# Eleven units of three heads instead of sixteen of two, in a kernel of two interleaved memory-attention layers

## The chip, the core and the metric

The kernel runs on one core of a Trainium2 chip. A core has five engines that run their own instruction streams and wait for each other through semaphores: TensorE (PE, matrix products; PEld is its weight loads), VectorE (DVE), ScalarE (ACT), GpSimd (POOL) and SyncE (SP, which only issues transfers). The metric is the time of one execution on the device in microseconds. Three timed runs of the kernel before took 1757.47 us in the median (1755.57 to 1760.67).

## The reference

A model of two layers, each an attention with a recurrent memory and then a gated feed-forward, on 2048 tokens of width 512, in bf16:

```python
def _A_ref(x, mem0, Wq, Wk, Wv, Wo, seg_len):      # 32 heads of 128, M = 8 memory rows, seg_len = 32
    mem = mem0
    for s in range(n_seg):                          # 64 segments, one after another
        h = jnp.concatenate([mem, xs], axis=1)      # 8 + 32 = 40 rows
        q, k, v = h Wq, h Wk, h Wv                  # per head
        scores = jnp.where(mask, q k^T * scale, -1e9)
        o = softmax(scores) v, then Wo
        mem = o[:, :M, :]; outs.append(o[:, M:, :])
def _B_ref(x, w_gate, w_up, w_down):
    return (_sigmoid(x w_gate) * (x w_up)) w_down   # hidden width 1792
x = x + A(layernorm(x)); x = x + B(layernorm(x))    # layer 1
x = x + A(layernorm(x)); x = x + B(layernorm(x))    # layer 2, same weights
```

The memory rows that a segment's attention puts out are the first rows of the next segment, so the 64 segments of a layer are a chain.

## The kernel before, in words

Both layers run interleaved: layer 2 follows layer 1 by `LAG` = 6 segments. There are 70 steps; step t does segment t of layer 1 and segment t - 6 of layer 2, side by side as 80 columns (2 x 40). The first six and the last six steps have one layer only, 40 columns. `emit_step` (line 743) writes one step. All attention weights stay in SBUF; the feed-forward weights stream from HBM by GpSimd (lines 1037, 1038, 1062) every time `ffn` (line 998) handles a block of four segments.

**A step.** The 32 heads are taken in six groups (line 379): a unit is the pair of heads k and 16 + k, a group is three units, and the last group is one unit. For each group: Q and K of three heads at a time (line 820, four matmuls per head and matrix), a ScalarE copy to `qku`, the scores (line 855), then on VectorE and ScalarE mask, maximum, difference, exponential, sum, reciprocal and product (lines 869 to 886). The product goes to `pb`, each head in 64 columns of which 40 are used, so that two heads side by side fill 128. One transpose per unit (`ptr`, line 898) turns [80 x 128] into [128 x 80], also in one-layer steps, where only 40 of the 80 columns are wanted.

Then the two heads of a unit have to be kept apart for one common matmul with V. Two copies, `spread` (line 903), write `ptsb` as a block diagonal: the first takes rows 0 to 39 as they are, the second takes rows 0 to 103 with a per-row factor (`self.lower`, 0 for rows below 64, 1 above), so that zeros stand above the second head's block. `pvm` (line 925) multiplies: per unit and layer one matmul with 104 rows (40 + 24 unused + 40) and 80 columns, the weights being a piece of `vsb`. The result is copied to `otsb`, and line 943 adds Wo over all heads in one bank, `WB`. The memory rows in it are copied (lines 956, 961) into `hT` for the next step.

**V rows.** `vsb` has on its rows the keys of a segment: 40 for the first head of each unit, from row 64 on 40 for the second, and 1024 columns (eight heads) per half; a step takes two halves out of a ring of three (`NV`, line 421). The rows have two sources. V of most input rows is known long before: `v_pass` (line 599), `v_half` (636) and `v_strip` (666) compute it for whole blocks, and write it to a scratch tensor `scr` in HBM; line 789 reads it back, per layer and half two transfers, eight in a two-layer step. V of the memory rows and eight input rows is computed in the step itself by `strips` (line 724, matmuls at line 734), copied to the tile `sst`, and spread from there by line 800, one transfer per layer and block of eight heads, again eight in a two-layer step. All of line 789 and 800 are issued by SyncE. PV of a unit waits for both kinds in its half.

**Order.** Nothing is scheduled at run time. `trace` puts down all tasks with what they read and write; `plan` (line 242) takes their order from the packed text `SEQUENCE`, which also has one bit for each task that may run on either of two engines (ACT or DVE, or SP or POOL). Each engine then executes its tasks in that order. `replay` works out from modelled durations how transfers are paced; `warm` (line 325) puts matmuls on zeros (`hot`, line 1162) into modelled gaps early on. PSUM has eight banks, shared by all products.

At the beginning `load_weights` (line 488) brings Wv, then Wq, Wk and Wo in three batches of heads, while x blocks are normalised and their V rows go to the scratch.

Of the kernel before, what the change touches and what calls it, by code (L numbers as in the profile page):

```python
# [19 lines left out]
P = 128  # L20
# [33 lines left out]
;Az(@{9OPHfC}>o!3$&_>1cSGYy1w~*vKE?LoDUO!`XV%;;<878Kns_@I+iX(74V;U`D{e|Ct%0x6blOT;$DygtQ>WP_y0Zcs7M#8ZgxUzzs1BnG}%%cF5wibfz3Qe?%`=oGh%zVh=;yB58Og*`2$-%qT7YV)FI3#cQ^-I`x  # L54
&G{OfvfRK6T<NC@t+QdCx)4z22oURtuAXpAF|V^CA{0!Ao{;`#`yj1}i}Ch1r!j#UV(;CNGol)x2h`J)DP9<BIpIsggIr#a!ba?+s&P#^RrmvVPy2*cyt7ch@zX6gEG&YI)o)JH5iL)7^9(PB6)!dAz;Y>UB@c<YVrN*C$bk
`UBwxs%kJ&?H?qYss(T75_dqsan*LzmQ){N;jUfw1c#CWqehzA$bo--AB9!AL8|W%F))ViX;pkqiEd(%YsDHo*bQ+Dg|=KU)AQj+ks~~@3^wm`_dZc8XZ*mz}(B-?_G(C#8p|4$Q#jx3XS>_o;hPB%dYQC+~oqb=g0I%bKtG
rSyhjEKC+rbuKFU;PbVGyzF>7DXS4Dk(aL?0A6S7iKWJkuCsaZ&wNS??_ECKySWtgC`xDEZU7C!<AWxdzXj9U63NE>5Yc6MUM!7}k$&z&CD4Mla1DpWf(QeoFAc7y6O-ohA*ItoS2?=lJ@>LMq|C7o-Q8n#{?T6q|_($+pX6
_0p%s=*z9d@;E{BD!r4PB$D?4z4z;XM@A#gsbsw%iD9{;3M*L!&6|ltPpFZQTPfqi^op#C!}qxPUz6u}3{jgHF!ebPiVZgXqS03CQ8v-k^3u$xlzD)_nJq?>hx&T8b)Jx{V$$2*B5>5^-kIDbQ&(GA|hBP)=(F?%hkS#wDGT
#CgyK0Y5|l(;pl7Bm@Ae`Cyw<S6@#gvE3~Ltq-@hCG>dDXcDc%GIkP2+V$B{Y>_nQ!q=}&Y+eo3QV2~`flzV#9vZJ2FD(Zk$8y(4#}Gzn2=SG;2y@jmsXC~$pqizsS*wm@&w7Uemq&=!vw#M0gE>GU>#$Al_0&=9s7POC5w8
wCVt2dTrQcn;ydUO5caqQt6VFB?-M8;1Ij6Y~M34Ev7kYUxYI$|K2JNpoTCmkHk{v}Wa!DAN((%u!t;57gvoi1te}1KiaM<<Va7#z02ym&DO$`u$X-wNEhOCQmVMW5<OAt7`JQGSmyI;Fyvnh!4?T{@zS!O)ZV>{z{r&tN&O  # L60
GBcSt6qX}d8a@4cOwmdsxK@1Mv#YW7t`b1`tw8V7V$oq81-WwoNwK3hAbp_&Ys1}c-<U=_9c;uuhJNYdr`2njZZKcwlt>88tzHvO<Nw5)Ia)x)ih?ng+Q@u-1OY<8L7mfOLpjHniZZD8P~1DNqhyvLy*LY_DO!$iQvIF_03_
EE9^VE0M=lc09iWqK)*H(FN&wXUGRX5gsbTWY``n1P4gcn)QJkM!Iu6;e3IY1dX)C1c=g)b8a@WC_r^F=YXB~yd>RICxRDT#R?s3pwyYelZ~(Od=uW_AQ|iZ{J?O2Am?k$-NCs+M8c1q6!k?FG0iDOdDLy%rHBg8)hQ4+1-z
R@{Ap_p0pz2P$nvy9rmW#FlW6F73m@h@<*e%j$nj_5%VAco?ETMr0eZ8Xy!ug=sl2$=fEr(So8hOJjcF6~Y#gB(6Vk!U4p28BbPQF;9$eSp3>(2rofD%eIS4Bc`-i8r`jjAPY>>>+KN(2@?36~@jFQW+GNvKz@40>EqjZYO|
77iYTi^gp5gp<lX+CRHkg_c+NPMgLuKp~|RIx%VhyA`P5<f^cxq>-JHS#&X5OH08lau6tLMOd>6r9lh*>|n+|+zk|ZVu}uQCdbU|W0?3WPkvHZ05nA&gswskrIp9CwZvW<S;hgUNw8j9H~ri&@R3`gYkPqser(Gw_2?=sq;T
y!hDzC8@%U)2fOR|h!v&I<K``c))TWKf3ngkKJ8>2Px^zg{R-tySFsSs(ViW4Mg5E8eo;c0H_qUP>?X8C3ZLi2Y>4oZp*rb^2xUJpiPqU1@@f!(!Z)ujbMCs8jDY(7I2P#e*mF`S@c#VZ<oZF}8WM<UftqDN4%J*(@+;wKru
&(Tm7u}Lr!6j(z$eS-xqe=3E7~&mY%i~Pr0J>Z)oX3f4M3a>RN4NT){|o2~R2gALm^t!8(ySW99ZkQ1^Mcvtk<kcIG;)P3;TII7uxp3TN|Op2#w{XqT5mmQW)a7oA=p7LL4FK9k9=P=qkq>Wz=Mx2PY99!w^_{^AvWc3$n%)
j;66<cd`~YkPDsPxCgft~&{c40sfzWb8^PRKCrLGR2ZwGeABQkk-tfoQtzz~DB(L@wF2kmrai9Yz9rw=m(z7Zw4~vQWSOjZ#;%i!*8A}~%D<yc5shh!vHK(ToI(Scm4-?@}3ByBLIf*T)P{h5e1`3IDo283%H7tZ0Y2N$!;`
# [293 lines left out]
class Kern:  # L361
    def __init__(self, ctx, tc, x_in, mem0, Wq, Wk, Wv, Wo, w_gate, w_up, w_down, out, lag=6, ring=8):
# [14 lines left out]
        assert ring > lag and lag >= BLK + 1  # L377
        self.NSTEPS = self.NSEG + lag
        self.scale = float(DH) ** -0.5
        self.HH = H // 2  # L380
        self.groups = []
        for u in range(0, self.HH, 3):
            us = list(range(u, min(u + 3, self.HH)))
            self.groups.append(([h for k in us for h in (k, self.HH + k)], us))
# [103 lines left out]
    def load_weights(self):  # L488
# [10 lines left out]
        for h0, n in ((0, 4), (4, 4), (8, 4), (12, 4), (16, 4), (20, 4), (24, 4), (28, 4)):  # L499
            cs = slice(h0 * P, (h0 + n) * P)  # L500
            tk = ld(self.wv[:, :, cs], wv_v[:, :, cs], P * self.DC * n * P * 2, [("wv", h) for h in range(h0, h0 + n)], [("wv", h0 - 8)] if h0 > 4 else [])
            if h0 > 4:
                tk.after = pl.writer[("wv", h0 - 8)]
# [738 lines left out]
```

## Time and profile before

| | |
|---|---|
| median of three timed runs | 1757.47 us |
| profiled execution, device time | 1760.81 us |
| its span, first to last instruction | 1759.0 us |
| instructions | 92161 |
| TensorE clock granted | 1.00 |
| moved by transfers | 273.42 MB, 155 GB/s |
| transposes, line 898 | 1120 |
| PV matmuls, line 925 | 2048 |
| scratch reads into `vsb`, line 789 | 508 |
| strip transfers into `vsb`, line 800 | 516 |

How to read a page. A line of groups has the source line, the engine and operation, what is written and read, the count, then busy time and the mean length of one in ns. Matmuls overlap in the pipeline, so the mean length of one (some 200 ns) isn't what it costs: that is the distance between starts, which the timeline shows. A line of waits has who waited, for whom, us in total, times, and the longest. SPq and POOLq are the queues of SyncE and GpSimd. Windows (from:to in us) give each engine's busy time in a stretch. "issue" as a releaser means that nothing in the profile explains the idle time.

### The profile page before, as it was taken

To read this page: it belongs to the slowest core of one execution; us is meant where nothing else is said; L and a number is where in the kernel's file an instruction comes from. 1 tells how busy PE (TensorE), PEld (TensorE's weight loads), DVE (VectorE), ACT (ScalarE), POOL (GpSimd) and SP (SyncE) were. 2 spreads that over 40 slices of the span, in tenths; PEclk is the share of its full clock that TensorE was granted. 3 is DMA by queue.
4 is the path that set the end of the run, shared out by engine and by line. 5 is a ranking of instruction groups with operands and counts; after the bars stand their busy time and mean duration, and the time that the engine had idled before them with its cause. 6 is when DMAs were issued, how large, how long until landed. Compare 5 with 4: busy or idle time off the path is not lost.

```text
span 1759.0 us, 92161 instructions
## 1 busy us (share of the span) xinstructions
PE 1742.0 (99%) x40015; PEld 1503.4 (85%) x40015; DVE 1233.3 (70%) x4096; ACT 1113.6 (63%) x2946; POOL 570.8 (32%) x818
## 2 busy tenths in 40 slices
PE   9999999999999999999999999999999999999998
PEld 4688788888898888989898888988888898988887
DVE  6577777676767776776677667667766776677766
ACT  4576777666566655666666667656666666666564
POOL 4312133423233233323333242323234232332433
PEclk9999999999999999999999999999999999999999
DMA  8934455645555455545555463545456454554554
GB/s 292 311 105 131 119 165 149 194 128 141 142 153 155 139 167 142 171 119 157 152 153 164 133 194 105 158 141 175 127 157 186 131 151 133 151 164 126 158 151 127
DMA packets 136128, 273.42 MB, mean 155 GB/s; under 512 B 30706, under 2 KB 69498, under 8 KB 135722
## 3 DMA queue, kind: packets, MB, share of 16 engines
q0 software_dynamic: 55680, 180.73, 35.5%
q1 hardware_dynamic: 80042, 86.79, 17.2%
q8 instruction: 314, 5.14, 1.3%
q14 instruction: 92, 0.75, 0.1%
HBM read 221.78 MB, written 27.07 MB: 141 GB/s over the span
## 4 chain that ended last, share of the span: by engine, by line
PE 94%; DMA 3%; SPq 1%; issue 1%; DVE 0%; ACT 0%; POOL 0%; DVEq 0%; POOLq 0%; ACTq 0%
PE bank L820 33%; PE bank L943 17%; PE bank L1045 11%; PE bank L734 7%; PE bank L609 7%; PE bank L1068 6%; PE bank L855 4%; PE bank L925 4%; PE bank L898 2%; PE bank L569 1%; DMA wq_sb<-in_A_Wq_dram 1%; DMA vsb<-sst 1%; SPq L800 1%; DMA wk_sb<-in_A_Wk_dram 1%; PE bank L1013 0%
## 5 line engine op out<-in xcount | busy, mean ns | idle before, releaser
L820 PE MATMUL bank<-hT,wk_sb 128*128 128x80 bf16 (+3 forms) x8960 | 616.2, 198 | 4.5 <-issue 3.1
L820 PE MATMUL bank<-hT,wq_sb 128*128 128x80 bf16 (+3 forms) x8960 | 615.9, 198 | 2.8 <-DMA wq_sb<-in_A_Wq_dram 1.5
L1176 ACT CAST qku<-bank 128x480 bf16<-128x480 f32 (+4 forms) x770 | 383.5, 507 | 272.8 <-PE bank L820 244.5
L820 PEld LDWEIGHTS <-wq_sb 128*128 128x128 bf16 x8960 | 453.7, 99 | 30.7 <-issue 14.0
L820 PEld LDWEIGHTS <-wk_sb 128*128 128x128 bf16 x8960 | 447.1, 99 | 4.0 <-issue 2.5
L869 DVE TENSOR_TENSOR st<-bank,cst 40x240 f32<-40x240 f32 (+3 forms) x768 | 280.1, 368 | 122.5 <-PE bank L855 108.2
L943 PE MATMUL bank<-otsb,wo_sb 128*128 128x80 bf16 (+1 forms) x8960 | 363.2, 198 | 0.6 <-issue 0.6
L943 PEld LDWEIGHTS <-wo_sb 128*128 128x128 bf16 x8960 | 335.1, 99 | 11.4 <-issue 1.3
L1062 POOL DMA_DIRECT2D wd<-in_B_w_down_dram x217 | 154.7, 713 | 354.6 <-PE bank L1068 85.6
L1038 POOL DMA_DIRECT2D wu<-in_B_w_up_dram x217 | 164.4, 758 | 298.9 <-PE bank L1045 94.3
L1176 ACT CAST otsb<-bank 128x480 bf16<-128x480 f32 (+3 forms) x420 | 199.9, 483 | 93.8 <-PE bank L925 58.3
L1037 POOL DMA_DIRECT2D wg<-in_B_w_gate_dram x217 | 164.0, 756 | 244.0 <-PE bank L1045 108.2
L879 ACT ACTIVATE st<-st 80x240 f32<-80x240 f32 (+3 forms) x420 | 158.9, 381 | 66.2 <-DVE st L876 63.1
L1045 PE MATMUL bank<-xnT,wg 128*128 128x128 bf16 (+2 forms) x1784 | 171.7, 218 | 0.5 <-issue 0.5
L1045 PE MATMUL bank<-xnT,wu 128*128 128x128 bf16 (+2 forms) x1784 | 171.1, 218 | 0.0
L881 DVE TENSOR_REDUCE small<-st 80x6 f32<-80x240 f32 (+3 forms) x420 | 151.0, 361 | 24.8 <-ACT st L879 22.2
L855 PE MATMUL bank<-qku 128*128 128x80 bf16 (+1 forms) x2240 | 160.7, 198 | 0.4 <-ACT qku L1176 0.4
L876 DVE TENSOR_TENSOR st<-st,small 80x240 f32<-80x240 f32 (+3 forms) x420 | 154.5, 370 | 6.6
L886 DVE TENSOR_TENSOR pb<-st,small 80x240 bf16<-80x240 f32 (+3 forms) x420 | 153.8, 370 | 6.1
L874 DVE TENSOR_REDUCE small<-st 80x6 f32<-80x240 f32 (+3 forms) x420 | 151.6, 363 | 6.7
L925 PE MATMUL bank<-ptsb,vsb 104*128 104x80 bf16 x2048 | 139.3, 199 | 2.2 <-DMA vsb<-sst 1.6
L855 PEld LDWEIGHTS <-qku 128*128 128x128 bf16 x2240 | 114.2, 99 | 30.1 <-ACT sst L1176 5.5
(107 smaller groups left out, 2330.7 us busy)
## 6 DMA issues: line engine op xcount, KB each, us to landing
wg<-in_B_w_gate_dram POOLq DMA_DIRECT2D x220, 256.0 KB, 4.3
wu<-in_B_w_up_dram POOLq DMA_DIRECT2D x220, 256.0 KB, 4.3
wd<-in_B_w_down_dram POOLq DMA_DIRECT2D x220, 256.0 KB, 4.0
vsb<-scr SPq DMA_DIRECT2D x460, 48.0 KB
vsb<-sst SPq DMA_DIRECT2D x464, 32.0 KB
scr<-vst SPq DMA_DIRECT2D x120, 96.0 KB
wv_sb<-in_A_Wv_dram SPq DMA_DIRECT2D x8, 512.0 KB
wo_sb<-in_A_Wo_dram SPq DMA_DIRECT2D x10, 384.0 KB
```

Source lines behind the costliest of these rows:

```text
L820: nc.tensor.matmul(o_ap, lhsT=W[:, c, h * P:(h + 1) * P], rhs=mv(c), start=(c == 0), stop=(c == DC - 1))
L855: nc.tensor.matmul(s_all(SB)[:, w0 + i, :], lhsT=fview(qku[:, i, 0, 0:1], [(1, P)]), rhs=qku[:, i, 1, 0:ncol], start=True, stop=True)
L869: pl.add("DVE", dve_ns(n, True), lambda gsz=gsz, hs=hs, st=st, SB=SB, pj_=pj_, npj_=npj_, mk=mk, idx=idx: nc.vector.tensor_tensor(out=st[p ...
L876: pl.add("DVE", dve_ns(n), lambda gsz=gsz, hs=hs, st=st, mx=mx: nc.vector.tensor_tensor(out=st[pr, hs], in0=st[pr, hs], in1=mx[pr, hs].uns ...
L879: pl.add("ACT", act_ns(n), lambda hs=hs, st=st: nc.scalar.activation(out=st[pr, hs], in_=st[pr, hs], func=ACTF.Exp, scale=self.scale), r=s ...
L925: nc.tensor.matmul(fview(OB[:, o:o + 1], [(ncol, 2), (1, L)]), lhsT=self.vsb[halves[u // 8]][0:64 + L, j, (u % 8) * P:(u % 8 + 1) * P], rh ...
L943: nc.tensor.matmul(WB[:, c * ncol:(c + 1) * ncol], lhsT=self.wo[:, h, c * P:(c + 1) * P], rhs=otsb[:, hl, 0:ncol], start=(h == 0 and c == ...
L1037: pl.add("POOL", 760, lambda wg=wg, fs=fs: nc.gpsimd.dma_start(out=wg[:], in_=self.wgv[:, :, fs]), r=[("wo", self.H - 1)], w=[gk] + bt, la ...
L1038: pl.add("POOL", 760, lambda wu=wu, fs=fs: nc.gpsimd.dma_start(out=wu[:], in_=self.wuv[:, :, fs]), r=[("wo", self.H - 1)], w=[uk] + bt, la ...
L1045: nc.tensor.matmul(gu[:, 2 * i + k, 0:n], lhsT=W[:, c, i * P:(i + 1) * P], rhs=xnT[:, c, rw], start=(c == 0), stop=(c == DC - 1))
L1062: pl.add("POOL", 760, lambda wd=wd, ip=ip: nc.gpsimd.dma_start(out=wd[:], in_=self.wdv[:, 2 * ip:2 * ip + 2, :]), w=[dk] + (["boot"] if se ...
L1176: nc.scalar.copy(out=dst, in_=src)
```

## The change

Units have three heads: k, 11 + k and 22 + k. There are eleven; the last has two heads. A group has two units, so group sizes stay six heads, five times, and then two. `pb` has three heads of 40 columns side by side (120 of 128); one transpose per unit, of as many columns as the step has. `spread` runs once per head place of the unit, three times in a full group, the second and third scaled by their own 0/1 factor. PV has 120 rows and 120 columns. `vsb` has one whole buffer per step (11 x 128 columns), two of them; its rows have no gap, so the filling with zeros at the beginning goes away.

V is stored in an order of its own: the first eight heads of each of the three rows, then the remaining 3, 3 and 2. `runs` cuts a stretch of stored columns into pieces that are contiguous in the scratch. Scratch reads are one transfer per layer and row, and strip transfers two (k = 0 for the first eight units, k = 1 for the others); both may be issued by SyncE or GpSimd, as a bit in the new sequence says. The sequence is new as a whole.

```diff
+        self.NU = (H + 2) // 3
+        self.row_heads = [list(range(i * self.NU, min((i + 1) * self.NU, H))) for i in range(3)]
         self.groups = []
-        for u in range(0, self.HH, 3):
-            us = list(range(u, min(u + 3, self.HH)))
-            self.groups.append(([h for k in us for h in (k, self.HH + k)], us))
+        for u in range(0, self.NU, 2):
+            us = list(range(u, min(u + 2, self.NU)))
+            self.groups.append(([r[k] for k in us for r in self.row_heads if k < len(r)], us))
...
-        self.NV = 3
+        self.NV = 2
-        self.vsb = [c.tile([P, 2, 1024], BF16, name=f"vsb{i}") for i in range(self.NV)]
+        self.vsb = [c.tile([P, 2, self.NU * P], BF16, name=f"vsb{i}") for i in range(self.NV)]
-        self.pb = [c.tile([LW, HG, 64], BF16, name=f"pb{i}") for i in range(3)]
-        self.ptsb = [c.tile([P, HG, 2, L], BF16, name=f"ptsb{i}") for i in range(3)]
+        self.pb = [c.tile([LW, 2, P], BF16, name=f"pb{i}") for i in range(3)]
+        self.ptsb = [c.tile([P, 2, 2, 3, L], BF16, name=f"ptsb{i}") for i in range(3)]
...
-        nc.vector.memset(self.lower, 1.0)
-        nc.vector.memset(self.lower[0:64], 0.0)
+        for i in (1, 2):
+            nc.gpsimd.memset(self.lower[i], 1.0)
+            nc.gpsimd.affine_select(out=self.lower[i], in_=self.lower[i], pattern=[[0, 1]],
+                                    compare_op=ALU.is_ge, fill=0.0, base=-i * L, channel_multiplier=1)
...
-        for k, t_ in enumerate(self.vsb):
-            pl.add("ACT", 1760, lambda t_=t_: (t_[32:64], fview(self.hot[32:64, 0:1], [(0, 2), (0, 1024)])),
...
+    def runs(self, k, w):
+        out = []
+        for i, r in enumerate(self.row_heads):
+            n = len(r) - 8
+            for p0, m, s0 in ((0, 4, 8 * i), (4, 4, 8 * i + 4), (8, n, 24 + 3 * i)):
+                lo, hi = max(s0, 4 * k), min(s0 + m, 4 * (k + w))
+                if lo < hi:
+                    h = r[p0 + lo - s0]
...
+                        out.append(((lo - 4 * k) * P, h * P, (hi - lo) * P, keys))
...
-        full = slice(0, LW)
+        full = slice(0, ncol)
...
-            for hf, vh in enumerate(halves):
-                for i in range(0 if j and not s else 2):
...
-                    pl.add("SP", 430, lambda j=j, s=s, row=64 * i + row + lo, h0=h0, vh=vh, r0=s * XS + lo, nx=nx: nc.sync.dma_start(
...
+            for i, rh in enumerate(self.row_heads):
...
+                pl.add(("SP", "POOL"), {"SP": 430, "POOL": 590}, lambda j=j, row=L * i + row + lo, h0=rh[0], m=m, r0=s * XS + lo, nx=nx: (
+                    "dma", self.vsb[vh][row:row + nx, j, 0:m], self.scr[j][r0:r0 + nx, h0 * P:h0 * P + m]),
...
+            for k in (0, 1):
...
+                    for i in range(3):
+                        p0, o, m, c = (32 * i, 0, self.full, 0) if not k else (96, 3 * P * i, (len(self.row_heads[i]) - 8) * P, self.full)
+                        pl.add(("SP", "POOL"), {"SP": 632, "POOL": 640}, lambda p0=p0, o=o, m=m, c=c, i=i, j=j, lo=lo, k0=k0, nr=nr: (
...
-                           r=kk, w=[(qku, "e")], use=[qku])
+                           r=kk + hkeys, w=[(qku, "e")], use=[qku])
...
-                    nc.tensor.transpose(out=pt[:, ul * LW:(ul + 1) * LW], in_=pb[full, 2 * ul:2 * ul + 2, :].rearrange("p i k -> p (i k)"),
+                    nc.tensor.transpose(out=pt[:, ul * LW:ul * LW + ncol], in_=pb[full, ul, :],
                                         identity=self.ident[full, full])
...
-            for i in (0, 1):
+            for i in range(ni):
                 def spread(i=i, nu=nu, ptsb=ptsb, PB=PB):
-                    r = slice(0, 64 * i + L)
+                    r = slice(0, L * (i + 1))
...
-                                         lhsT=self.vsb[halves[u // 8]][0:64 + L, j, (u % 8) * P:(u % 8 + 1) * P],
-                                         rhs=ptsb[0:64 + L, ul * nj + idx, :, :], start=True, stop=True)
+                                         lhsT=self.vsb[vh][0:L * ni, j, u * P:(u + 1) * P],
+                                         rhs=ptsb[0:L * ni, ul, idx, 0:ni, :], start=True, stop=True)
```

`load_weights` also changes: Wv comes in ten pieces in the new stored order instead of eight, and Wq, Wk and Wo in batches of 2, 4 and 5 units, each as three pieces, one per row of heads. In `v_pass`, `v_half` and `v_strip` each write to the scratch becomes one write per piece that `runs` returns.

306 lines of the change are left out of this document (159 added, 147 removed).

## The prediction

> **What bounds the kernel now.** First the page's busy shares and the table by stage, to see which engine has no room left; the last columns are granted clock, DMA share and GB/s.
>
> ```profile
> PE 1742.0 (99%) x40015; PEld 1503.4 (85%) x40015; DVE 1233.3 (70%) x4096; ACT 1113.6 (63%) x2946; POOL 570.8 (32%) x818
> ...
> 0.00:90.00 90.00, 84.76 (x1125) 48.14 (x1126) 53.01 (x159) 47.50 (x115) 34.57 (x78) 1.00 0.91 296
> 90.00:195.00 105.00, 103.61 (x2828) 86.58 (x2826) 79.93 (x289) 73.43 (x255) 17.79 (x26) 1.00 0.40 113
> 195.00:1630.00 1435.00, 1430.99 (x32605) 1264.01 (x32602) 1010.74 (x3338) 921.82 (x2340) 472.77 (x651) 1.00 0.53 151
> 1630.00:1759.00 129.00, 122.66 (x3470) 104.63 (x3466) 89.60 (x312) 70.81 (x237) 45.69 (x63) 0.99 0.50 143
> ```
>
> TensorE is busy in 1431 of the 1435 us of the two-layer steps, at the full clock; only the first 90 us (DMA share 0.91) and the last 40 have holes. A busy engine need not be at its peak, so next the timeline of TensorE in a step's tail (start, length, line, count):
>
> ```profile
> 915.37 0.39 PE L1045 MATMUL bank<-xnT,wu 128*128 128x128 bf16 x4
> 915.59 0.60 PE L925 MATMUL bank<-ptsb,vsb 104*128 104x80 bf16 x12
> 916.02 0.28 PE L898 MATMUL bank<-cst,pb 80*128 80x80 bf16 x3
> 916.14 0.39 PE L1045 MATMUL bank<-xnT,wg 128*128 128x128 bf16 x4
> ...
> 918.49 0.28 PE L898 MATMUL bank<-cst,pb 80*128 80x80 bf16 x3
> 918.60 1.02 PE L943 MATMUL bank<-otsb,wo_sb 128*128 128x80 bf16 x24
> 919.46 0.38 PE L925 MATMUL bank<-ptsb,vsb 104*128 104x80 bf16 x6
> ```
>
> From start to start: 24 matmuls of 80 columns take 0.86 us (35.8 ns each), 12 of line 925 take 0.43 (35.8), three transposes 0.12, 4 of 128 columns 0.22 (55.5). In the one-layer steps 48 Wo matmuls of 40 columns take 1.21 us (1644.77 to 1645.98), 25.2 each. So TensorE issues without holes and columns are what it pays for. Third, the waits of TensorE:
>
> ```profile
> PE bank L820 <- issue: 4.0, 6, 1.6
> PE bank L925 <- DMA vsb<-sst: 1.6, 3, 0.9
> PE bank L820 <- DMA wq_sb<-in_A_Wq_dram: 1.5, 1, 1.5
> PE bank L820 <- DMA wk_sb<-in_A_Wk_dram: 1.2, 1, 1.2
> ```
>
> All its waits together are some 13 us in 1759. There is little stall to win: a gain must come out of TensorE's own work, and any new stall counts in full.
>
> **The change, part by part.** The profiled execution took 1760.81 us, its span being 1759.0; the three timed runs have the median 1757.47, 3.3 less. Differences are worked out on the span and set against the median. There are 58 two-layer steps and 12 one-layer ones.
>
> Transposes (line 898): sixteen a step become eleven. In a two-layer step all keep 80 columns: 5 x 35.8 = 179 ns saved. In a one-layer step they shrink to 40 columns; no transpose of that size is in the trace, the bounds are the 40-column Wo matmul (25.2) and no shortening (35.8). I take 25.2: 16 x 35.8 - 11 x 25.2 = 296 ns.
>
> PV (line 925): 32 matmuls of 80 columns become 20 of 120 and 2 of 80; the columns stay 2560. No row has 120 columns; between 35.8 (80) and 55.5 (128) the line gives 52.2. 32 x 35.8 - 20 x 52.2 - 2 x 35.8 = 30 ns a step (bounds -36 at 55.5 each and, at 50 for bare columns, 74); in a one-layer step half, 15. The contraction grows from 104 rows to 120; Wo with 128 rows costs the same 35.8, so nothing.
>
> Saved: 58 x 209 + 12 x 311 = 12.1 + 3.7 = **15.8 us**; with the bounds of both, 58 x 143 + 12 x 161 = 10.2 to 58 x 253 + 12 x 333 = 18.7. QK, scores, Wo, feed-forward and strip matmuls keep count and shape.
>
> Spreads (lines 1168, 1170, 1176, 1178): two per full group become three of two thirds the size, two of them scaled. Rows now: plain 240 elements 348 ns on ScalarE and 266 on VectorE, 120 elements 247 and 206; scaled 460 and 333, 120 elements 360 and 262. On the line between, 160 elements cost 281 and 226 plain, 393 and 286 scaled. With the present split of 70:30 a group goes from 323 + 422 to 265 + 2 x 361, +242 ns; times 290 groups 70 us, and some 16 more for the 60 one-layer groups: +86 us on engines that are busy 2347 of 3518. Average room is no cover, so the place: in the tail the transposes end near 918.6, both spreads run on VectorE (0.34 and 0.26 long, 918.88 to 919.39), and PV follows at 919.46 under 24 Wo matmuls. A third spread adds 0.1 to 0.2 us there, while the transposes are 36 ns shorter. If the cover is the same, 58 x 0.1 = 6 us at most likely, 12 at the upper end; feed-forward matmuls (four of line 1068 stand at 922.2) can be put there, then nothing. I take **+1.5**.
>
> V rows: per two-layer step 8 transfers from scratch become 6, 8 strip transfers become 12. Over the run 508 become 381 and 516 become 774; scratch writes (lines 624, 660, 671) grow by some 95, because the last eight stored heads come from three rows. That is about 230 more issues of 0.4 to 0.65 us, some 125 us over SyncE and GpSimd. Do they arrive in time? SyncE's timeline in the same step:
>
> ```profile
> 907.25 3.74 SPq L800 DMA_DIRECT2D vsb<-sst  x6
> 911.04 1.36 SPq L789 DMA_DIRECT2D vsb<-scr  x1
> 912.44 1.14 SPq L800 DMA_DIRECT2D vsb<-sst  x2
> ```
>
> 0.62 us each. On SyncE alone, the six for stored columns 0 to 1023 leave by 911.0; the chain shows 3.5 us for one that TensorE waited for at 207, so they land by 914.5, and first PV is at 915.59: 1.1 us to spare. The other six leave by 914.7, land by 918.2, and are now first wanted by the fifth group (old pace about 919.5), where before the second half was wanted by the third (917.62). Any share on GpSimd makes this earlier, if its queue is free. Zero, with -1.6 (all waits on strips gone) and +58 x 0.27 as ends.
>
> [...]
>
> Two whole V buffers instead of three halves: SyncE no longer stands before half of a step's scratch reads until the step before has finished with it.
>
> ```profile
> SPq L789 <- PE bank L925: 264.4, 62, 11.0
> SPq L800 <- DVE sst L1178: 214.2, 33, 14.3
> ```
>
> The first row mostly goes; the second, waiting for the strip's copy, becomes what SyncE stands in, and what is queued behind it (scratch writes, x loads) is not wanted soon. Nothing on TensorE.
>
> Start: line 671 runs four writes in the chain ahead of the Wq load and now has six: 2 x 0.65 = 1.3 us at most, zero if GpSimd or the order takes them past; two more Wv pieces, and 27 instead of 24 loads of Wq, Wk and Wo, move the same bytes. The three ACT fills of V buffers (1.9 us each, 14 to 29 us) go, off the path. Four small POOL operations at the beginning lie beside the first x load (4.2 us). I take **+0.7**, ends 0 and +4. The six `load` steps' copy that now also waits for the step's columns stands ahead of a copy that needs QK of these columns anyway: nothing.
>
> Sum: 1757.5 - 15.8 + 1.5 + 0.7 = **1744** (-0.8%); its own range 1738 to 1752.
>
> **Rivals.** (1) Softmax engines take the tail. VectorE already runs without a hole from 914.9 to 918.6; if the third spread and its engine time push each two-layer step's last groups by 0.2 to 0.3 us, 58 x 0.25 = 14 us return: 1744 + 14 = 1758, no change. For it: the order written out must place filler exactly there. Against it: some 4 us of feed-forward matmuls a step can be placed freely.
>
> (2) Slower: strip transfers stand in GpSimd's queue behind a weight issue that waits for a matmul.
>
> ```profile
> POOL wd L1062 <- PE bank L1068: 85.6, 36, 11.7
> POOL wd L1062 <- PE bank L855: 74.9, 17, 13.3
> POOL wd L1062 <- PE bank L898: 62.5, 24, 34.7
> ```
>
> The second of these waits 4.4 us on average. With 1.1 us to spare, a strip caught behind it is 3.3 us late, and first PV with it. Eight such steps of 58 cost 26 us: 1744 + 26 = 1770; from 0.27 us a two-layer step (five such) it eats the gain. Against it: the order is fixed and could place the issue after the strip.
>
> (3) Pairs of weight load and matmul bind, not columns: then fifteen pairs fewer a two-layer step at 35.8 save 537 ns, ten in a one-layer step 358: 31.1 + 4.3 = 35.4, so about 1722. Against it: 25.2, 35.8 and 55.5 ns for 40, 80 and 128 columns. [...]
>
> (4) The change does not do what it says: if the start and end swallow the one-layer savings (3.7 us, where DMA and the serial chain rule) and spreads a further 3, 1751.
>
> **How the numbers follow.** About 0.3% (5 us) is what a measurement of this kernel tells from no change. The forecast has 0.52, rival (4) 0.12, (3) 0.01: faster 0.65. Rival (1) has 0.14, of which I put 0.08 within 0.3% and 0.06 beyond it, where the stall per step passes 0.33 us; rival (2) 0.21. So same 0.08, slower 0.27. Range: the lower end is the forecast's own, 1738 (0.04 below); above, (1) lies inside and (2) is cut at its price, 1770 (0.15 beyond). I forecast a gain because the removed work is on the one engine without holes, and every cost is on engines with room.
>
> **What would show it.** Right: line 898 has 770 matmuls (132 of 40 columns, at some 25 ns), line 925's successor 1408 at some 52; a two-layer step 0.2 us shorter; TensorE's waits still near 13 us. Wrong: waits of PV on V transfers above 15 us, on GpSimd-issued ones above all (rival 2); waits of weight loads of PV on spreads, or tails with PE idle (rival 1); TensorE's busy time unchanged with many warm-up fills (line 1162), meaning holes in the plan that were filled.

## The result: 0.5% slower

The changed kernel takes 1766.73 us in the median of six executions (1765.00 to 1767.42), the kernel before 1757.72 in six (1755.57 to 1761.14): a ratio of 1.0047, 95% interval 1.0033 to 1.0060. The forecast was 1744, the time lies inside its range and on the wrong side of the kernel before. The profiled executions, on which all that follows is worked out, took 1767.42 us (span 1765.4) and 1760.81 (span 1759.0), and on the spans the sum had -15.8 + 1.5 + 0.7 = -13.6 us where +6.4 came out: 20 us have to be found.

Lines of the changed kernel: transposes are line 928 (before: 898), PV 955 (925), Q and K 848 (820), scores 883 (855), Wo 973 (943), strips 759 (734), gate and up 1075 (1045), down 1098 (1068), V pass 634 (609). All transfers of V rows and scratch writes are recorded at line 1202.

First the page's busy shares and the table by stage of the changed kernel (columns as before: stretch, length, PE, PEld, DVE, ACT, POOL with counts, clock, DMA share, GB/s):

```profile
PE 1745.5 (99%) x39037; PEld 1495.3 (85%) x39037; DVE 1249.7 (71%) x4196; ACT 1137.7 (64%) x3191; POOL 857.4 (49%) x1371
...
0.00:90.00 90.00, 81.46 (x946) 44.87 (x946) 48.41 (x142) 38.99 (x106) 48.77 (x109) 0.98 0.90 292
90.00:195.00 105.00, 104.00 (x2776) 85.07 (x2773) 77.55 (x274) 75.69 (x287) 33.20 (x54) 1.00 0.41 113
195.00:1630.00 1435.00, 1428.72 (x31823) 1256.66 (x31822) 1031.78 (x3467) 942.83 (x2520) 714.62 (x1117) 1.00 0.54 151
```

TensorE is as "busy" as it was, with 978 matmuls fewer. GpSimd has gone from 570.8 to 857.4 us. Now the groups of the two lines that were to bring the gain, by shape, and the waits of TensorE:

```profile
L955 PE MATMUL bank<-ptsb,vsb 120*128 120x120 bf16 x1280 | 122.3, 216 | 4.7 <-DMA vsb<-scr 2.2 <-issue 1.7
L928 PE MATMUL bank<-cst,pb 80*128 80x80 bf16 x638 | 78.4, 201 | 0.1
L928 PE MATMUL bank<-cst,pb 40*128 40x40 bf16 x132 | 15.2, 184 | 0.1
```

```profile
PE bank L634 <- DMA wv_sb<-in_A_Wv_dram: 3.5, 4, 1.1
PE bank L955 <- DMA vsb<-scr: 2.2, 3, 1.4
PE bank L955 <- issue: 1.7, 1, 1.7
PE bank L848 <- DMA wk_sb<-in_A_Wk_dram: 1.6, 2, 1.3
PE bank L973 <- DMA wo_sb<-in_A_Wo_dram: 1.5, 1, 1.5
```

The counts are those of the forecast: 638 + 132 = 770 transposes, 1280 + 128 = 1408 PV matmuls. The waits come to 15.2 us in all against 12.4 before. None of these lines shows a loss of 20 us. What places it is the end of each step, which VectorE marks in its timeline by the copy of the new memory rows from `WB` into `hT` (lines 956 and 961 before, 986 and 991 after). Between such marks (us, worked out from the two traces):

| stretch | before | after | difference | forecast |
|---|---|---|---|---|
| to the end of step 0 | 79.7 | 84.0 | +4.3 | +0.4 |
| steps 1 to 5, one layer | 90.2 | 93.6 | +3.4 | -1.6 |
| steps 6 to 62, two layers | 1438.1 | 1435.6 | -2.5 | -10.4 |
| steps 63 to 68 (five of one layer) | 115.8 | 117.5 | +1.7 | -1.8 |
| the rest | 35.2 | 34.7 | -0.5 | -0.3 |

So three different things went wrong: one-layer steps, which were to become shorter, became longer by 0.3 to 0.7 us each; two-layer steps gained a quarter of what they should; the start is late.

The stretches do not hold quite the same work in the two kernels. In the changed one twelve more products of the V pass (line 634, 512 columns, 216 ns each, 2.6 us) stand in step 0 and eleven fewer in steps 1 to 5; 32 more gate and up products (1.8 us) stand in steps 6 to 62 and 32 fewer in steps 63 to 68. So part of the late start is work done earlier, and the one-layer steps at the end got longer by more than the table shows, some 0.7 us each. In steps 1 to 5 of this trace a stretch of 3.4 us at half clock (granted 0.50 from 83.9 to 87.3 us) adds some 1.4 us (four QK products take 180 ns there and 100 behind it). And one execution is a coarse measure: steps 6 to 62 with the two-layer steps of the kernel before took 1438.1, 1435.8 and 1435.3 us in three traces (before, e3_before_short, h2_before_matmul), so that the gain there may be nothing.

**One-layer steps.** The timeline of TensorE in step 64, after:

```profile
1642.88 0.31 PE L883 MATMUL bank<-qku 128*128 128x40 bf16 x6
1643.12 0.21 PE L928 MATMUL bank<-cst,pb 40*128 40x40 bf16 x2
1643.27 0.40 PE L1075 MATMUL bank<-xnT,wg 128*128 128x128 bf16 x4
...
1644.68 0.26 PE L848 MATMUL bank<-hT,wk_sb 128*128 128x40 bf16 x4
1644.86 0.21 PE L928 MATMUL bank<-cst,pb 40*128 40x40 bf16 x2
1645.01 0.27 PE L848 MATMUL bank<-hT,wq_sb 128*128 128x40 bf16 x4
```

Six score matmuls of 40 columns need 6 x 25 = 0.15 us, so the transposes could start at 1643.03; they start at 1643.12. Two of them at 25 ns would be done by 1643.17; the next matmul starts at 1643.27. At the second place the same: 4 x 25 after 1644.68 is 1644.78, they start at 1644.86 and hold TensorE until 1645.01. Nothing is waited for, and no line of waits has it. Over all 59 such pairs the median is 92 ns of nothing ahead of the pair and 147 ns from its first start to the next matmul, 239 in all, where a pair of 80 columns in the two-layer steps takes 77 with no gap ahead. With the 12 single ones (93 and 122) the 71 visits hold TensorE for 17.1 us (from distances between starts, less what the matmul ahead needs by its columns); the 192 long transposes of the kernel before cost 6.9.

The kernel before had a gap of that size in sight, at another line. Its timeline around a strip (line 734, 32 columns of the array):

```profile
924.89 0.31 PE L820 MATMUL bank<-hT,wk_sb 128*128 128x80 bf16 x4
925.13 1.91 PE L734 MATMUL bank<-wv_sb,hT 128*32 128x512 bf16 x32
```

Four matmuls of 80 columns from 924.89 end at 925.03, the strip starts 0.1 us later and waits for nothing. That was the row nearest to a matmul which uses a part of the array only.

**Two-layer steps.** PV matmuls follow each other within a visit at 52 ns in the median (1280 of 120 columns), as forecast. But between the first and the last of a visit TensorE waits more: 24 distances over 90 ns with 7.4 us above the 52 ns, against 14 with 3.5 us before (11 with 1.9 in e3_before_short, whose two-layer steps are the same). The two largest, after:

```profile
692.62 0.22 PE L955 MATMUL bank<-ptsb,vsb 120*128 120x120 bf16 x1
694.53 0.32 PE L955 MATMUL bank<-ptsb,vsb 120*128 120x120 bf16 x3 [1.69 <-issue]
...
795.54 0.22 PE L955 MATMUL bank<-ptsb,vsb 120*128 120x120 bf16 x1
797.13 0.32 PE L955 MATMUL bank<-ptsb,vsb 120*128 120x120 bf16 x3 [1.37 <-DMA vsb<-scr]
```

Both end with the landing of a scratch read that SyncE issued, by the semaphores that these matmuls wait for (694.34 and 796.99 us). SyncE's timeline has them as the last of a row of V transfers, the second within the four from 789.48:

```profile
687.36 1.77 SPq L1202 DMA_DIRECT2D vsb<-sst  x3
689.18 1.37 SPq L1202 DMA_DIRECT2D vsb<-scr  x1
...
789.48 3.73 SPq L1202 DMA_DIRECT2D vsb<-scr  x4
```

From issue (689.18 and 792.91) to landing they took 5.2 and 4.1 us; the forecast had reckoned with 3.5 from a single row, that of a strip transfer. The chain that ends in the second wait (start, length, what) shows why the fourth read left so late:

```profile
788.39 4.44 DMA scr<-vst
...
792.91 4.08 DMA vsb<-scr
```

It left when a write to the scratch had landed. The four largest distances, at 493.6, 692.6, 795.5 and 1202.2 us, lie in steps 18, 26, 30 and 46, in which layer 2 begins a block of four segments and reads rows of a new block for the first time; steps of this kind hold 5.1 of the 7.5 us of such waits in the whole trace. Whether the scratch writes come too late there or too much stands on the queues was not tried.

**The start.** SyncE in the changed kernel, and the DMA engines in three stretches of 5 us:

```profile
61.11 2.21 SPq L1202 DMA_DIRECT2D scr<-wg  x2
65.03 2.34 SPq L1202 DMA_DIRECT2D vsb<-scr  x2
67.42 0.41 SPq L505 DMA_DIRECT2D wo_sb<-in_A_Wo_dram  x1
67.94 0.59 SPq L1202 DMA_DIRECT2D vsb<-sst  x1
68.58 4.54 SPq L505 DMA_DIRECT2D wo_sb<-in_A_Wo_dram  x6
```

```profile
60.00:65.00 5.00, 3.09 (x49) 1.92 (x46) 3.34 (x11) 1.95 (x5) 2.91 (x6) 1.00 1.03 345
65.00:70.00 5.00, 4.94 (x99) 3.41 (x100) 2.97 (x11) 3.70 (x12) 0.00 (x0) 1.00 0.41 133
70.00:75.00 5.00, 5.00 (x33) 2.33 (x31) 2.97 (x12) 4.02 (x12) 2.16 (x5) 1.00 0.94 287
```

Two reads of V rows stand ahead of seven Wo loads and hold SyncE until 67.42; the DMA engines run half empty (0.41 from 65 to 70; before it was 1.09 there). The last piece of Wo then is 1.5 us late for line 973.

### The profile page after: what moved, and what is told of

Same layout as the page of the kernel before. It is cut to its first block, busy times and chain, and to the rows that moved or that the text cites. A ratio compares the mean times of both kernels' runs of the same rounds, so it can differ in the third digit from the quotient of the medians.

```text
span 1765.4 us, 91641 instructions
## 1 busy us (share of the span) xinstructions
PE 1745.5 (99%) x39037; PEld 1495.3 (85%) x39037; DVE 1249.7 (71%) x4196; ACT 1137.7 (64%) x3191; POOL 857.4 (49%) x1371
## 4 chain that ended last, share of the span: by engine, by line
PE 91%; DMA 4%; issue 2%; SPq 1%; POOL 1%; ACT 1%; DVE 0%; DVEq 0%; ACTq 0%; POOLq 0%
PE bank L848 32%; PE bank L973 17%; PE bank L1075 11%; PE bank L759 7%; PE bank L634 6%; PE bank L1098 5%; PE bank L955 4%; PE bank L883 4%; PE bank L928 2%; DMA wv_sb<-in_A_Wv_dram 1%; DMA wk_sb<-in_A_Wk_dram 1%; PE bank L594 1%; DMA vsb<-scr 1%; DMA wo_sb<-in_A_Wo_dram 1%; SPq L505 1%
## 5 line engine op out<-in xcount | busy, mean ns | idle before, releaser
L1202 POOL DMA_DIRECT2D vsb<-sst x358 | 181.4, 510 | 139.4 <-ACT sst L1206 69.9
L1198 ACT ACTIVATE ptsb<-bank,small 80x160 bf16<-80x160 bf16 (+3 forms) x506 | 178.5, 376 | 21.6 <-PE bank L928 17.6
```

The costliest lines, as they stand in the source:

```text
L1198: nc.scalar.activation(out=dst, in_=src, func=ACTF.Copy, scale=by)
L1202: {"SP": nc.sync, "POOL": nc.gpsimd}[tk.on].dma_start(out=got[1], in_=got[2])
```

## Experiments

Each is compared with the kernel before on the same chip, whose medians there were 1754.81 (first four), 1755.22 (next four), 1755.34 (g) and 1755.94 us (h). Executions of one kernel differ by up to 9 us (19 in g1_all_sp), so ratios rest on 4 to 12 executions of the kernel named (one for e4_sweep, which has no ratio) and 11 to 29 of the kernel before; stretches between marks, from one profiled execution each, are good to 2 or 3 us. Theory A is that matmuls on few rows make TensorE pause, theory B that late V rows, spreads and the start took the gain.

### Transposes alone

e1_long: the changed kernel with 80 columns in all transposes.

```diff
-        full = slice(0, ncol)
+        full = slice(0, LW)
-                    nc.tensor.transpose(out=pt[:, ul * LW:ul * LW + ncol], in_=pb[full, ul, :],
+                    nc.tensor.transpose(out=pt[:, ul * LW:(ul + 1) * LW], in_=pb[full, ul, :],
```

> The changed kernel, with the transposes of the one-layer steps back at 80 rows and 80 columns (two lines); units of three and everything else stay. Theory A, few rows make TensorE switch: in the changed kernel's trace a visit of two transposes with 40 rows costs 92 ns before it and 147 ns itself, 239 in all, where two with 80 rows cost 77; for 60 visits of two and 12 of one that is 60 x 162 + 12 x 173 = 11.8 us, so 1766.7 - 11.8 = 1755, just below the kernel before, and no time before the transposes. Theory B, the loss is in late V rows and spreads and the start: the transposes get 132 x 10.6 ns longer, 1768.

Measured: 1757.28 us, ratio 1.0013 (1.0003 to 1.0022). Steps 1 to 5 took 88.5 instead of 93.6 us, steps 63 to 68 114.4 instead of 117.5, steps 6 to 62 1434.8 instead of 1435.6. Lengthening the transposes made the kernel faster, by 0.0034 of the time, about 6 us; it is still not faster than before.

e2_matmul: the one-layer transposes as plain products with the identity, 80 rows in, 40 columns out.

```diff
+                    if both:
                         nc.tensor.transpose(out=pt[:, ul * LW:ul * LW + ncol], in_=pb[full, ul, :],
                                             identity=self.ident[full, full])
+                    else:
+                        nc.tensor.matmul(PB[:, ul * L:(ul + 1) * L], lhsT=pb[0:LW, ul, :], rhs=self.ident[0:LW, 0:L], start=True, stop=True)
...
+                    if not both:
+                        pt = PB[r, 0:nu * L].rearrange("p (u j q) -> p u j q", u=nu, j=1)
```

The last two lines let the spreads read the product, which lies in the bank as fp32, where the kernel reads its transposes as bf16.

> The changed kernel, with the one-layer steps' transposes made as plain matmuls against the first 40 columns of an 80 x 80 identity: 80 rows in, 40 columns out, in fp32. Theory A says that the rows make the switch, not the columns: each costs 25 ns and no time before, 27 ns less per visit of two than in e1_long, so 1.7 us less than that: 1753. If it is the few columns that cost, it stays at 1767. Theory B: 1767.

Measured: 1755.88 us, ratio 1.0006 (0.9997 to 1.0016); h0_e2_again, the same kernel in a later comparison:

> e2_matmul once more, unchanged, as the yardstick for the two kernels beside it and for how much the start differs between executions: ratio to the kernel before 1.0006, end of step 0 between 84 and 86 us.

1758.76 us, ratio 1.0010 (0.9997 to 1.0022), end of step 0 at 83.7 us (84.3 in the first). Its 40 columns cost what the forecast had put down for 40 columns. From the timeline of e2_matmul:

```profile
1644.53 0.27 PE L960 MATMUL bank<-ptsb,vsb 120*128 120x120 bf16 x2
1644.64 0.21 PE L932 MATMUL bank<-cst,pb 80*128 80x40 bf16 x2
1644.70 0.46 PE L978 MATMUL bank<-otsb,wo_sb 128*128 128x40 bf16 x12
```

No gap ahead (2 x 52 ns after 1644.53 is 1644.64) and 0.06 us for two. So 40 columns are as cheap as forecast as long as 80 rows are used; the rows are left as the cause.

e3_before_short: the kernel before, with only its one-layer transposes cut to 40 rows and columns.

```diff
-        full = slice(0, LW)
+        full = slice(0, ncol)
-                    nc.tensor.transpose(out=pt[:, ul * LW:(ul + 1) * LW], in_=pb[full, 2 * ul:2 * ul + 2, :].rearrange("p i k -> p (i k)"),
+                    nc.tensor.transpose(out=pt[:, ul * LW:ul * LW + ncol], in_=pb[full, 2 * ul:2 * ul + 2, :].rearrange("p i k -> p (i k)"),
```

> The kernel before, with the short transposes alone: 40 rows and 40 columns in one-layer steps, still sixteen units of two. Theory A: a visit of three takes 92 + 2 x 39 + 108 = 278 ns instead of 112, so 60 x 166 + 12 x 173 = 12 us more than before: 1769.6. Theory B: fewer columns, 192 x 10.6 ns = 2 us less: 1755.5.

Measured: 1762.88 us, ratio 1.0043 (1.0030 to 1.0055). A visit of three costs 87 ns of gap and 172 ns instead of 112. This one edit, which my sum had at a gain of 2 us for this kernel (192 x 10.6 ns), costs 8, nearly as much as the whole change; theory A had the cause, with too large a size.

e4_sweep: the changed kernel with 40, 56, 64, 68, 72 and 80 rows and columns in its one-layer steps, by step.

```diff
-        full = slice(0, ncol)
+        full = slice(0, LW if both else (40, 56, 64, 68, 72, 80)[t % 64])
...
-                    nc.tensor.transpose(out=pt[:, ul * LW:ul * LW + ncol], in_=pb[full, ul, :],
+                    nc.tensor.transpose(out=pt[:, ul * LW:ul * LW + full.stop], in_=pb[full, ul, :],
```

> The changed kernel, with 40, 56, 64, 68, 72 and 80 rows and columns in the transposes of the six one-layer steps at the start, and again at the end. Theory A with a limit at half of the array: 40, 56 and 64 rows show some 92 ns before a visit and 80 ns after it, 68 and more show none. If the cost grows as rows are left out, 56 and 64 stand between. Time about 1766.7 - 6 = 1761 under the limit.

One execution, 1765.63 us, where some 1761 were expected; one execution can't decide on that. Gap ahead and time of a pair, medians in ns: 40 rows 93 and 147, 56 rows 93 and 154, 64 rows 87 and 161; 68 rows 0 and 63, 72 rows 0 and 68, 80 rows 0 and 77. Its timeline at 64 and at 68 rows, each behind two PV matmuls:

```profile
1689.25 0.27 PE L955 MATMUL bank<-ptsb,vsb 120*128 120x120 bf16 x2
1689.45 0.23 PE L928 MATMUL bank<-cst,pb 64*128 64x64 bf16 x2
1689.61 1.38 PE L973 MATMUL bank<-otsb,wo_sb 128*128 128x40 bf16 x48
...
1708.76 0.27 PE L955 MATMUL bank<-ptsb,vsb 120*128 120x120 bf16 x2
1708.87 0.23 PE L928 MATMUL bank<-cst,pb 68*128 68x68 bf16 x2
1708.93 0.39 PE L1075 MATMUL bank<-xnT,wg 128*128 128x128 bf16 x4
```

The step lies between 64 and 68 rows, and its price is some 90 ns on the way in and 95 on the way out (147 ns less the 54 of e2_matmul's pair; 161 less the 63 at 68 rows gives 98). What TensorE does in that time is not shown. Rows and columns of a transpose change together in this run, and no plain product of 64 rows or fewer stands in any trace here, so what is shown is shown for transposes. Plain products on 32 or 64 columns of the array have such a gap too: 95 ns in the median ahead of 72 runs of strips (line 759, 32 columns) and of four of line 672 (64 columns), in the changed kernel.

h2_before_matmul: the kernel before with e2_matmul's edit (product with the identity instead of the one-layer transposes, `rhs=self.ident[full, 0:L]`).

> The kernel before with its one-layer transposes as plain matmuls by the identity (80 rows in, 40 columns out), as e2_matmul has them: how much of what e2_matmul shows is this edit alone. At 27 ns instead of 36 each, 12 x 16 of them: 1.7 us less, ratio 0.999. If they cost what short transposes cost, 1.004.

Measured: 1755.94 us, ratio 0.9999 (0.9991 to 1.0008). A visit of three takes 80 ns instead of 112, as expected, and steps 1 to 5 88.6 us instead of 90.2; in the whole time 1.7 us can't be told from nothing.

### Late V rows

f2_no_v_wait: e2_matmul, where PV takes its weights from Wq's rows.

```diff
-                                         lhsT=self.vsb[vh][0:L * ni, j, u * P:(u + 1) * P],
+                                         lhsT=self.wq[0:L * ni, j, u * P:(u + 1) * P],
```

> e2_matmul, but PV multiplies by rows of Wq, which lie in memory from the start, in place of V rows: all V transfers still run, nothing waits for them, and the output is not attention's. Theory V (late V rows are what the two-layer steps still lose: 23 waits inside PV visits that sum to 5.7 us, against 2.1 before): steps 6 to 62 take 1428 us instead of 1433.4, the time is 6 us under e2_matmul, ratio to the kernel before 0.997. Rival (softmax groups are late anyway, and the same time is waited elsewhere): steps 6 to 62 stay within 1.5 us of 1433.4, ratio 1.000.

Measured: 1748.60 us, ratio 0.9959 (0.9947 to 0.9971); no PV distance over 90 ns is left inside a visit, and steps 6 to 62 take 1426.8 us instead of 1433.4. Against e2_matmul that is 0.0047, some 8 us. The edit takes away more than PV's waits: transfers into `vsb` no longer wait until PV has left the buffer. SyncE waits 142.7 us for that in e2_matmul (264.4 in the kernel before) and not at all in f2_no_v_wait and f3_before_no_v_wait.

f3_before_no_v_wait: the same edit in the kernel before (`lhsT=self.wq[0:64 + L, j, u * P:(u + 1) * P]`).

> The kernel before with the same edit: PV multiplies by rows of Wq in place of V rows (104 of them), the transfers still run. Theory V: only some 2 us of waits go, ratio 0.9985, steps 6 to 62 at 1436 instead of 1438.1; so without any V wait the three-head units are ahead by 8 us there. Rival (V rows cost both kernels alike): as much goes as from the three-head kernel.

Measured: 1752.98 us, ratio 0.9987 (0.9979 to 0.9996): 2 us; steps 6 to 62 take 1433.8 us. So the new V transfers, PV's waits for them and their own for PV together, cost the kernel some 6 us more than the old ones did (3 to 9 by the intervals). They don't cost both kernels alike.

g1_all_sp and g2_all_pool: e2_matmul with all V transfers on one queue.

```diff
         self.replay(order)
+        self.fixed, pace = self.warm(order), [tk.pace for tk in T]
...
+        for tk in T:
+            if tk.what == "vrow":
+                tk.on = "SP"
+        self.replay(order)
+        for tk, p in zip(T, pace):
+            tk.pace = p
```

> e2_matmul with every transfer of V rows issued by SyncE; places in the sequence, warm-up matmuls and the points that weight loads wait for stay. Rival 2 (strips are late in GpSimd's queue, behind weight issues): the V waits fall, 3 us under e2_matmul, ratio to the kernel before 0.999. Theory Q (the rows are late on either queue, because each has more transfers to issue than before and stands in order; one queue makes it worse): SyncE issues some 20 transfers a two-layer step instead of 11, the last ones leave later; 5 us or more over e2_matmul, ratio 1.0035 or more, PV waits above 10 us.

Measured: 1859.53 us, ratio 1.061 (1.058 to 1.065).

> e2_matmul with every transfer of V rows issued by GpSimd, else as in the run with all on SyncE. Rival 2: all of them stand behind weight issues that wait for matmuls; 15 us or more over e2_matmul, ratio 1.009 or more. Theory Q: as for SyncE, 5 us or more, ratio from 1.0035, and weight loads of the feed-forward late as well. If it is not slower than e2_matmul, neither queue's load is what makes rows late.

Measured: 1789.06 us, ratio 1.019 (1.017 to 1.021). The waits of TensorE in the two (PV is line 969 in both; 603 are the transposes behind the layernorm, 1089 gate and up), first all on SyncE:

```profile
PE bank L969 <- DMA vsb<-sst: 45.0, 26, 5.0
PE bank L969 <- DMA vsb<-scr: 22.4, 13, 4.8
PE bank L969 <- issue: 5.8, 4, 3.2
```

then all on GpSimd:

```profile
PE bank L603 <- DVE xn L594: 12.4, 9, 3.2
PE bank L1089 <- DMA wg<-in_B_w_gate_dram: 6.4, 6, 1.9
PE bank L969 <- DMA vsb<-sst: 5.5, 5, 3.2
PE bank L969 <- DMA vsb<-scr: 2.7, 3, 1.5
```

On SyncE alone the rows are late in step after step: 73 us of PV waits. On GpSimd alone they are nearly in time (8.9 us with `issue`), but what GpSimd does besides is late: the layernorm's power operation, without which `xn` isn't made, and the weight loads. So the split in the sequence is worth 33 us or more over either queue; strips behind weight issues (rival 2) are not what made the rows late.

h1_rerouted: e2_matmul with 47 V transfers on the other queue and eight moved; TensorE, VectorE and ScalarE run the same instructions in the same order. The edit is a new `SEQUENCE` text.

> e2_matmul with 47 of the 1155 V-row transfers on the other queue (24 to GpSimd, 23 to SyncE) and eight transfers moved a little in the order, chosen so that rows that land more than 1 us late by the schedule's own accounts come earlier; TensorE, VectorE and ScalarE execute the same instructions in the same order. Theory Q (each queue's order, not the transfers themselves, makes rows late, so it can be mended by a better assignment): some 4 of the 8 us that f2_no_v_wait won, ratio 0.998, V waits in the two-layer steps half of those of e2_matmul. Rival (the lateness only moves to other steps): ratio 1.0006.

Measured: 1757.05 us, ratio 1.0003 (0.9993 to 1.0012), beside 1.0010 for e2_matmul again. The wait of 1.7 us at 687 is gone, the one at 789 falls to 0.9 from 1.1 and 1.5 in the two traces of e2_matmul, one at 487 grows; PV distances over 90 ns sum to 4.6 us over the norm, against 5.7 and 6.2 in these two. A fifth to a quarter of it can be moved away, less than the expected half, and the time can't tell it from no change.

### The third spread

f4_two_spreads leaves the third copy out; g4_no_v_wait_two_spreads does so in f2_no_v_wait.

```diff
                 def spread(i=i, nu=nu, ptsb=ptsb, PB=PB):
+                    if i == 2:
+                        return None
```

> e2_matmul with the third spread of each group left out (the rows of the third head stay zero, so its share of the output is missing). Theory V (spreads are covered by other work): at most 1 us, ratio 1.000. Rival 1 (VectorE and ScalarE take the tail of each step, the third spread costs 0.1 us or more a step): 6 us or more, ratio 0.997 or less, steps 6 to 62 at 1427.

Measured: 1753.60 us, ratio 0.9989 (0.9980 to 0.9997), 0.0017 or 3 us under e2_matmul: between the two theories' sizes.

> f2_no_v_wait with the third spread left out as well (PV by rows of Wq, the third head's share missing). If the third spread costs TensorE time of its own, another 2 to 3 us go: ratio 0.9942. Rival (it only cost while V rows were late too, since a group waits for the later of the two): ratio as f2_no_v_wait, 0.996; or more than 3 us, if V waits had covered spreads: 0.993.

Measured: 1746.27 us, ratio 0.9944 (0.9926 to 0.9962), 0.0015 under f2_no_v_wait, but the intervals overlap. The two losses seem to add. Where the 3 us lie isn't shown: without the third spread steps 6 to 62 get shorter by only 0.9 us (f4_two_spreads against e2_matmul) and 0.4 (g4_no_v_wait_two_spreads against f2_no_v_wait), the five one-layer steps from 63 to 68 by 1.2 and 1.4, and steps 1 to 5 not at all.

### The start

f1_two_bits: in e2_matmul, the two reads of V rows that hold SyncE go to GpSimd, at the place of the third Wo load; all else stays.

```diff
...
+        wo = [p for p, tk in enumerate(order) if tk.what == "wo"]
+        mv = [tk for tk in order[wo[1]:wo[2]] if tk.on == "SP" and tk.what == "vrow"]
+        for tk in mv:
+            tk.on = "POOL"
+        order = [tk for tk in order[:wo[2]] if tk not in mv] + mv + order[wo[2]:]
...
```

> The kernel with one-layer transposes as plain matmuls (e2_matmul) with one more edit: two transfers of V rows from scratch, which SyncE issues ahead of its last seven Wo loads and on which it stands from 63.3 to 67.4 us, are issued by GpSimd at the same place of the sequence; warm-up matmuls stay where they were. Theory S (the start is late because SyncE stands in front of Wo loads while the DMA engines run dry, share 0.41 from 65 to 70 us): the last Wo loads leave 4 us earlier, about 3 us of idle DMA time fill, the wait of 1.5 us for Wo and the stretch at half clock go; end of step 0 at 81 instead of 84.3 us, time 3 us under e2_matmul, a ratio to the kernel before of 0.999. Rival (the start is late from what lies before 60 us, the V pass waiting for Wv loads at 11 to 27 us): no change, ratio 1.0006.

Measured: 1756.00 us, ratio 1.0004 (0.9995 to 1.0012). In its trace Wo leaves from 63.05 and 65.65 us on, instead of 66.25 and 67.40 in that of e2_matmul (67.42 and 68.58 in the changed kernel), the DMA share from 65 to 70 us is 0.73 instead of 0.55 (0.41), and step 0 ends at 80.7 us. But the time is not 3 us under e2_matmul.

> f2_no_v_wait (PV multiplies by rows of Wq, so its output is not attention's) with the two transfers of f1_two_bits on GpSimd. Theory S (the earlier start of f1_two_bits is real, and late V rows gave it back): end of step 0 at 80 us or less, 2 to 3 us under f2_no_v_wait, ratio 0.9945. Rival (its early start was one execution's luck): ratio as f2_no_v_wait, 0.996.

Measured: 1747.22 us, ratio 0.9949 (0.9936 to 0.9961), 0.0010 under f2_no_v_wait, not to be told from it; step 0 ends at 81.9 us, in f2_no_v_wait at 82.1. Over all traces, step 0 ends at 79.6 to 80.3 us in the kernel before and its variants; at 83.1 to 86.2 in seven with units of three and V waits; at 80.7 and 80.8 where V reads had gone to GpSimd (f1_two_bits, g2_all_pool), at 87.9 with all on SyncE, and at 81.9 to 82.1 in the three without V waits. So with V waits the start is some 3 us later where V rows stand ahead of Wo on SyncE. Without V waits the same move changed it by 0.2 us, where 2 were expected; the place is supported, and that it alone makes the start late is not shown. That mending it shortens the whole was expected and is not shown either: the later steps give it back, or the gain is within the 1 to 2 us that these comparisons leave open.

## Why the prediction was wrong

**Transposes, one-layer steps: the step that failed.** "I take 25.2", with the bounds "the 40-column Wo matmul (25.2) and no shortening (35.8)". Both bounds were matmuls of 80 rows or more; neither of them, nor a third row, was one of 64 or fewer. Measured are 239 ns a pair instead of 50. The term was -3.7 us with PV's part; e1_long gives back 6 us by making the transposes long again. With the 80 columns kept it would have been a gain of 5 x 36 ns in each of 12 steps, 2 us. The forecast looked for the price under the number of columns, while the nearest row by use of the array, the strips, showed a gap of 0.1 us that nobody waited in. Without the short transposes the change is level with the kernel before (1.0013 and 1.0006), though still not faster.

**Transposes and PV, two-layer steps: right in the price of one.** Pairs at 77 ns (medians: 41 from the first start to the second, 35 to the next matmul) and PV at 52 ns are the forecast's sizes, shown in the trace; the 50 ns "for bare columns" behind its bound are near 120 times the 0.42 ns a column of the 512-column products (27 of line 609 in 5.87 us from 19.74 us on, kernel before); that fewer columns come out as less time when nothing else is in the way is seen between f2_no_v_wait and f3_before_no_v_wait, 7.0 us in steps 6 to 62 without V waits, of the 11.9 that the sum has there without spreads.

**V rows: "Zero" was wrong.** The step "On SyncE alone, the six for stored columns 0 to 1023 leave by 911.0 ... 1.1 us to spare" took SyncE's rate of issue for its queue: it left out that SyncE stands between them (in the changed kernel's trace 433.6 us for strips' copies, 145.4 for PV to leave a buffer, 9.6 for scratch writes to land) and that the new transfers stand in that same order. With all on SyncE the kernel loses 104 us, and even in the given split 6 us more than before. The landing that it used, 3.5 us from one row, was 4.1 and 5.2 where it mattered, both times for a transfer that SyncE issued. The upper end, 58 x 0.27 = 15.7 us, held it. For V rows that GpSimd issued the changed kernel's trace gives medians from issue to landing of 3.5 us (from scratch) and of 2.4 to 3.6 (strips, by size), for those of SyncE none, so a difference between the two queues is not shown.

**Rival (2)** had the effect, late V rows, and the wrong queue. It was priced at 26 us, and the measured 6 us alone would not have turned the sign. That the measured time lies inside the range which this rival's price closes is luck: short transposes, a good part of the loss, were no rival's.

**Rival (1), spreads:** 3 us, where the sum had 1.5 and the rival 14. In size it is nearer to the sum; that it comes in every two-layer step, as the rival had it, the marks don't show.

**Rival (3), pairs bind:** refuted, by 36 and 52 ns for 80 and 120 columns once more.

**Start: "+0.7, ends 0 and +4".** Measured +4.3 to the end of step 0, just over the upper end, of which 2.6 us are products of the V pass that stood in steps 1 to 5 before. For the rest V rows ahead of Wo on SyncE are supported (f1_two_bits), and not the counted issues. The pieces of Wv (waits of 3.5 us in line 634, none before) may have a share; that was not tried.

**Signs named in the forecast:** 770 transposes and 1408 PV matmuls, yes; PV at 52 ns, yes; 132 transposes "at some 25 ns", no; steps 0.2 us shorter, no (2.5 us over 57 steps, 0.04 each); waits near 13 us, yes (15.2), which shows that waits as the profile lists them were no test of it: the pauses around short transposes are in none of them.

What adds up, between the medians on the scale of ratios: -12.1 us saved in two-layer steps (the sum's own figure), +4 in one-layer steps (6 for short transposes, less the 2 for fewer of them), +6 V rows and +3 third spread give +1; measured are +8. What V rows don't explain of the start, some 2 us, is left out, as it is about what the moved products of the V pass account for. So about 7 us stay open, and the intervals of the measured terms, 2 to 3 us each, allow for part of that. The same shows with these causes gone: g4_no_v_wait_two_spreads, which has no short transposes, no V waits and no third spread, is 0.0043 or some 7.5 us under f3_before_no_v_wait, where the sum saves 15.8. By the distances between starts in these two traces transposes save 13.6 us of the 13.9 forecast and PV 0.3 of 1.9, while warm-up matmuls and scores take 1.4 and 1.6 us more (warm-up by columns: 9.5 us against 7.8 before, line 1192). Why PV and scores do so, and where the rest is, stays open.

No version beat the kernel before: the best that compute the whole, h2_before_matmul (0.9999), h1_rerouted (1.0003) and f1_two_bits (1.0004), are equal to it. What f2_no_v_wait and g4_no_v_wait_two_spreads show, 0.4 to 0.6%, is the most that units of three could bring if V rows came in time and two copies were enough; without V waits the kernel before gains 0.1% too (f3_before_no_v_wait).

## What to carry to other kernels

When an edit cuts the rows of a transpose to between 40 and 64 among matmuls of 120 and 128 rows, price the visit and not the instruction: here some 185 ns a visit on top in the trace, for 40 rows as for 64, while 80 rows with 40 columns cost nothing extra (0.06 us for two, no gap ahead). In the whole time 72 such visits cost 6 to 8 us more than those with 80 rows, some 80 to 110 ns each. A bound for an operation that the trace does not have should come from a row that uses the engine in the same way, not only from one with the same count. For transfers moved to another place in a queue's order, the time from issue to landing and the rate of issue (3.5 and 0.62 us in the forecast) didn't say here when they arrive; what stood ahead of them did (a scratch write of 4.4 us ahead of the read at 792.91), and a run with all on one queue shows it at once (73 us of PV waits in g1_all_sp, 8.9 in g2_all_pool).

## What the runs showed of the hardware

Transposes of 40, 56 and 64 rows cost some 90 ns before and 95 after a visit among matmuls of 120 and 128 rows, those of 68, 72 and 80 rows nothing (e4_sweep). Plain products on 32 or 64 columns of the array have 95 ns ahead of them (the changed kernel). No column of the profile has this time: TensorE's idle time stays at 0.1 us in the group of 132 transposes, because one is recorded as 184 ns long and so covers the pause; only distances between starts show it. And after a hole of TensorE within the first 90 us the granted clock fell for a while in some traces (1.5 us up to 82.3 us in the changed kernel, then 0.50 for 3.4 us from 83.9 us on) and not in others (1.25 us up to 64.2 us in the kernel before, with 1.00 in every stretch of 5 us from 60 to 90; 2.0 us in a wait for Wv in f1_two_bits, whose mean over the whole execution is 1.000).
